# Reordering a pair's round in a fused attention and two-MLP kernel: evictions ahead of maxima, scores ahead of the next first mixing

## The chip, the cores and the metric

One core of a Trainium2 chip runs the whole program in one launch. The metric is the device time of a run in microseconds (us). Engines are called by their short names: PE (TensorE, matmuls), ACT (ScalarE), DVE (VectorE), POOL (GpSimd), and SP, which here only issues transfers. Each engine works through its own instructions in the order in which the program was written.

## The reference, cut to what matters

```python
# 4 batches, 12 heads, 448 positions, head size 64
scores = scale * np.matmul(q, k.transpose(0, 1, 3, 2))
scores = np.einsum('bhij,hg->bgij', scores, w_pre)       # first mixing of heads
scores = scores - np.max(scores, axis=-1, keepdims=True)
attn = np.exp(scores)
attn = attn / (np.sum(attn, axis=-1, keepdims=True) + 1e-09)
attn = np.einsum('bhij,hg->bgij', attn, w_post)          # second mixing of heads
out = np.matmul(attn, v)
# then a gated MLP with a token mixing (w_in, w_sg, w_out), then a second MLP
# (w_theta, w_tok, w_ch); w_in and the others come as 64-bit floats
```

## The kernel before, in words

The program has an attention stage and then two dense stages. Only the attention stage is touched. It is written out by hand, with no scheduler: the order of the Python calls is the order of instructions on every engine.

The 448 query rows of a batch make four tiles, of 120, 120, 120 and 88 rows. A tile is cut into blocks of 10 rows, and two blocks make a **pair**; the last tile of a batch ends in a single block of 8 rows. That is 6 + 6 + 6 + 5 = 23 pairs a batch, 92 in all. The main loop runs one **round** r per pair and works on several pairs at once, at different depths:

- *re-layout* for pair r+4: SP moves a pair's rows of all heads from the score tile `s` into two `blk` tiles (L216). Three sets of `blk` take turns, so the copy waits for the first mixing of three pairs earlier.
- *first mixing* (`premix`) for pair r+2: PE multiplies `blk` by `kpre` into two psB banks (L224). There are two psB buffers, so it waits for the exponentials of the pair before.
- *maxima* (`rowmax`, DVE, L230, `nmx`) and *exponentials* (`expo`, ACT, L238, `e`, each followed by a small read of its sum), then a reciprocal: first step on POOL (`recip`, L244), second on DVE (`recip2`, L249), both writing `rc`. `weigh` (POOL, L260) scales the second mixing's weights `wr` by it for pair r+1.
- *second mixing* (`postmix`) for pair r: PE, 64 small matmuls into two of three psC buffers (L282; L274 for a single).
- *evictions* of psC: `at_hi` on ACT (L305, tile `ah`, half precision) and `at_lo` on DVE (L311, tile `al`, the remainder `psC - ah`, so it needs `ah` first). A pair has two of each, e = 0 and 1.
- *scores* for a later tile (`scores`, PE, L200, into psA, which is one buffer of two banks) and their eviction on ACT (L206, tile `s`). A tile has six score steps, spread over the 6 or 5 rounds of the tile ahead; over 5 rounds one round gets two.
- *products with v* (`attn_v`, PE, L334, into psD, one bank), scaled by DVE (`out_x`, L342) and stored by SP (`store_x`, L347).

What doesn't run in each round is put into lists by round number and run from them: `early` (transfers), `work` (scores, products with v, two small matmuls `v_turn` L149 and `v_spread` L160 per batch that also write psA, `out_x`) and `late` (preparing the next batch's v: `v_max`, `v_mul` L172, `v_hi` L177, `v_lo` L181; and the decoding of `w_in`). Decoding is cut into 18 jobs (the argument `extra`), spread over rounds 1 to 84, one about every 4.7 rounds. A job has `words` in round r (ACT `dp` L568 and `dl` L569, then DVE `da` L571 and L573), `value` and `high` in r+1 (DVE L579; ACT `dh` L584, DVE L585) and `low` in r+2 (DVE L591, POOL L593).

Between a round's list `late` and the next round stands the second remainder, `at_lo(r, 1)`:

```python
            for fn, a in late.get(r, []):
                fn(*a)
            if live:
                at_lo(r, 1)
```

Of the kernel before, what the change touches and what calls it, by code (L numbers as in the profile page):

```python
# [6 lines left out]
F32 = mybir.dt.float32  # L7
# [3 lines left out]
U32 = mybir.dt.uint32  # L11
AF = mybir.ActivationFunctionType
ALU = mybir.AluOpType
# [11 lines left out]
LR, LQ = 4, 2  # L25
# [6 lines left out]
def attention(tc, nc, io, xT, B, extra, tail):  # L32
# [8 lines left out]
    NR = len(pairs)  # L41
# [7 lines left out]
    with ExitStack() as es:  # L49
# [5 lines left out]
        def pool_r(name, bufs, **kw):  # L55
            return early_es.enter_context(tc.tile_pool(name=name, bufs=bufs, side="right", reuse_waits="tile", **kw))
# [5 lines left out]
        dec = pool_r("a_dec", 1)  # L62
# [155 lines left out]
        def premix(r):  # L218
            ps = mix[r] = [psB.tile([128, 512], F32, tag="psB", name="psB") for _ in sblk[r]]
            for h in range(2):  # L220
                k = slice(64 * h, 64 * h + 64)
                for e, blk in enumerate(sblk[r]):
                    c = 64 * (h ^ e)
                    nc.tensor.matmul(ps[e][c:c + 64, :S], kpre[k, e], blk[k], start=True, stop=True)  # L224
            del sblk[r]

        def rowmax(r):
            nmx[r] = sm_p.tile([128, 2], F32, tag="nmx", name="nmx")
            for e, ps in enumerate(mix[r]):
                nc.vector.tensor_reduce(out=nmx[r][:, e:e + 1], in_=ps[:, :S], axis=AX.X, op=ALU.max, negate=True)  # L230
# [68 lines left out]
        def at_hi(r, e):  # L299
            b, t = pairs[r][:2]  # L300
            if e >= len(pc[r]):
                return
            if r == first[b, t] and e == 0:
                at[b, t] = [at_p.tile([128, 4 * H * TI], F16, tag=tag, name=tag) for tag in ("ah", "al")]
            nc.scalar.activation(out=at_view(r, e, at[b, t][0]), in_=at_src(r, e), func=AF.Copy, scale=2.0 ** -17)  # L305

        def at_lo(r, e):
            if e >= len(pc[r]):
                return
            ah, al = (at_view(r, e, x) for x in at[pairs[r][:2]])  # L310
            nc.vector.scalar_tensor_tensor(out=al, in0=at_src(r, e), scalar=2.0 ** -17, in1=ah,  # L311
                                           op0=ALU.mult, op1=ALU.subtract)
# [34 lines left out]
            nc.sync.dma_start(out=dst.rearrange("(c p) i -> p c i", p=128), in_=xs.pop((b, t, half))[:, :, :n])  # L347


        early, work, late = {}, {}, {}  # L350

        def put(d, r, fn, *a):
            d.setdefault(r, []).append((fn, a))
# [5 lines left out]
        for T in range(1, nt):  # L359
            b, t = tiles[T]  # L360
            u = units(T)
            for c in range(NP):
                put(work, u[c], scores, b, t, c)
            if T > 1:
                put(early, u[0] - QO, load_q, b, t)
            if t == 0:
                for c, r in enumerate(units(T - 1)):
                    put(early, r, load_k, b, c)
        for b in range(B):
            f = first[b, 0]  # L370
            g = min(f, 1)
            for c in range(NP):
                put(early, f - 9 + c if b else -4 + c // 2, load_v, b, c)
                put(late, f - 7 + c if b else -2 + c // 3, v_max, b, c)
                for d, fn in enumerate((v_mul, v_hi, v_lo)):
                    put(late, f + 2 - g + c + d, fn, b, c)
            put(work, f - g, v_turn, b)
            put(late, f - g, v_top, b)
            put(work, f + 1 - g, v_spread, b)
            put(late, f + 1 - g, v_scale, b)  # L380
        for T in range(nt):
            b, t = tiles[T]
            for c in range(NP):
                if T == nt - 1:
                    r = last[b, t] + 1 + c // 3
                else:
                    r = last[b, t] + min(1 + c, 5 if t == 2 else 6)
                put(work, r, attn_v, b, t, c)
                if c % 3 == 2:
                    put(work, r, out_x, b, t, c // 3)  # L390
                    put(early, r + 1, store_x, b, t, c // 3)

        for j, fn in enumerate(extra):
            r = JR0 + (NR - JR0 - JR1) * j // len(extra)
            put(early, r - 2, fn[0], dec)
            for d, i in ((0, 1), (1, 2), (1, 3), (2, 4)):
                put(late, r + d, fn[i], dec)
            put(early, r + 4, fn[5], dec)


# [16 lines left out]
        for r in range(-LR, NR + 7):  # L417
            live = 0 <= r < NR
            if 0 <= r + LR < NR:
                relayout(r + LR)  # L420
            for fn, a in early.get(r, []):
                fn(*a)
            if live:
                postmix(r)
            if 0 <= r + LQ < NR:
                premix(r + LQ)
            if 0 <= r + LQ - 1 < NR:
                recip2(r + LQ - 1)
                weigh(r + LQ - 1)
            if live:  # L430
                at_hi(r, 0)
                at_lo(r, 0)
                at_hi(r, 1)
            if 0 <= r + LQ < NR:
                rowmax(r + LQ)
                expo(r + LQ)
                recip(r + LQ)
            for fn, a in work.get(r, []):
                fn(*a)
            for fn, a in late.get(r, []):  # L440
                fn(*a)
            if live:
                at_lo(r, 1)
            if r == NR - LR - 1:
                early_es.close()
            for key in (2 * (r - NR), 2 * (r - NR) + 1):
                for fn in tail.get(key, []):
                    fn()
# [21 lines left out]
class Dense:  # L470
# [71 lines left out]
    def decode(self, src, n, dst, tiles=None):  # L542

        nc, box = self.nc, {}

        def block(pool, i):
            if tiles:
                return tiles(i)  # L550
            if i == 0:
                box["hl"] = pool.tile([128, 2, 256], F32R, tag="dh", name="dh", bufs=self.out_bufs)
            return box["hl"][:, i, :n]

        def load(pool):
            raw = pool.tile([128, 256, 2], U32, tag="draw", name="draw", bufs=self.raw_bufs)
            nc.sync.dma_start(out=raw.rearrange("p n w -> p (n w)")[:, :2 * n], in_=src.bitcast(U32))
            box["raw"] = raw

        def words(pool):  # L560
            raw = box["raw"]
            lo, hi = raw[:, :n, 0], raw[:, :n, 1]
            a, low, p = (pool.tile([128, 256], F32, tag=t, name=t, bufs=self.mid_bufs)[:, :n]
                         for t in ("da", "dl", "dp"))
            au = a.bitcast(U32)


            nc.scalar.activation(out=p, in_=hi.bitcast(F32), func=AF.Copy, scale=2.0 ** -112)  # L568
            nc.scalar.activation(out=low, in_=lo, func=AF.Copy, scale=2.0 ** -52)  # L569
            pu = p.bitcast(U32)  # L570
            nc.vector.tensor_scalar(out=au, in0=pu, scalar1=3, scalar2=0x7FFFFFF8,  # L571
                                    op0=ALU.logical_shift_left, op1=ALU.bitwise_and)
            nc.vector.scalar_tensor_tensor(out=au, in0=pu, scalar=0x80000000, in1=au,  # L573
                                           op0=ALU.bitwise_and, op1=ALU.bitwise_or)
            box.update(a=a, low=low, p=p)

        def value(pool):
            a, p = box["a"], box["p"]
            nc.vector.tensor_scalar(out=p.bitcast(U32), in0=a.bitcast(U32), scalar1=0xFF800000, scalar2=None,  # L579
                                    op0=ALU.bitwise_and)  # L580

        def high(pool):
            h = block(pool, 0)
            nc.scalar.activation(out=h, in_=box["a"], func=AF.Copy)  # L584
            nc.vector.tensor_tensor(out=box["p"], in0=box["p"], in1=box["low"], op=ALU.mult)  # L585
            box["h"] = h

        def low(pool):
            a, p, h = (box[k] for k in ("a", "p", "h"))
            lo = block(pool, 1)  # L590
            nc.vector.tensor_tensor(out=a, in0=a, in1=h.bitcast(F32), op=ALU.subtract)  # L591
            eng = nc.vector if self.mid_bufs > 1 else nc.gpsimd
            eng.tensor_tensor(out=lo, in0=a, in1=p, op=ALU.add)  # L593
            box["lo"] = lo

        def store(pool):
            if tiles:
                return
            nc.sync.dma_start(out=dst, in_=box["hl"][:, :, :n].bitcast(F32))

        return load, words, value, high, low, store

    def decode_tiles(self, src, rows, c0, c1, tiles):
# [669 lines left out]
```

## Time and profile before

| what | value |
|---|---|
| median of 3 runs | 1001.59 us (1000.46 to 1003.74) |
| the profiled execution: its own time | 1002.4 us |
| its span, first to last instruction | 1000.5 us |
| busy over the span: PE, DVE, ACT, POOL | 92%, 68%, 53%, 25% |
| mean granted TensorE clock | 0.971 of full speed |

Times in the rows below are us from the span's start. A round shows best on ACT: it begins with the pair of `ah` evictions, of which most rounds have one row with x2. Counted so, round 0 begins at 30.77, round 4 at 52.87 and round 83 at 426.16. A row of the timeline has start, duration, engine, line, operation, output <- input, and in brackets how long the engine had been idle and what it waited for. Rows that follow each other closely overlap a little, since an engine starts an instruction before the one ahead has left it; the distance between two starts is what an instruction costs its engine. A row of the windows view has from:to, its length, then the busy time (and instructions) of PE, PE's weight loads, DVE, ACT and POOL, then the granted TensorE clock, the DMA engines' busy share and GB/s.

### The profile page before, as it was taken

Reading aid. Unit: us, or ns where it says so; the run is one execution under the profiler, and the core shown is the slowest. Engines: PE = TensorE matmul, PEld = TensorE weight load, DVE = VectorE, ACT = ScalarE, POOL = GpSimd, SP = SyncE. Lnnn points to the kernel's source line nnn. Section 1 sums busy time; section 2 is a strip of 40 time slices with the busy share of each in tenths; the row PEclk is TensorE's granted clock in tenths of the full one; section 3 lists DMA queues with packets and bytes.
Section 4 is the critical chain, followed back from the end, with each engine's and each line's share of the span. In section 5 each row is a group of like instructions: output and inputs, shape, how many; then the busy total and the mean of one; then the engine's idle time right before and its main releaser. Section 6 shows DMA issues by size and latency. Waiting matters only on the chain.

```text
span 1000.5 us, 28660 instructions
## 1 busy us (share of the span) xinstructions
PE 918.6 (92%) x11632; PEld 687.9 (69%) x11632; DVE 679.3 (68%) x1512; ACT 525.7 (53%) x1188; POOL 248.9 (25%) x450
## 2 busy tenths in 40 slices
PE   6888979988898978996989999998998999999998
PEld 2344545544554545555868888887988999999997
DVE  2576657756675757773999898976987737837521
ACT  4577657766576757763755546443553404513310
POOL 0152215311251225320000000001460623622611
PEclk9799989999899999998999999999999999999999
DMA  5537644666347634458635857679762031030111
GB/s 165 168 122 212 181 161 149 187 173 185 105 151 202 191 118 150 142 121 267 200 104 171 283 166 218 195 250 329 220 212 82 26 102 49 26 102 16 56 56 56
DMA packets 126963, 151.80 MB, mean 152 GB/s; under 512 B 26352, under 2 KB 112624, under 8 KB 126832
## 3 DMA queue, kind: packets, MB, share of 16 engines
q1 hardware_dynamic: 126832, 149.97, 48.2%
q8 instruction: 92, 1.51, 0.6%
q14 instruction: 39, 0.32, 0.1%
HBM read 79.09 MB, written 32.31 MB: 111 GB/s over the span
## 4 chain that ended last, share of the span: by engine, by line
PE 48%; DVE 21%; ACT 20%; issue 5%; DMA 4%; SPq 1%; ACTq 0%; DVEq 0%
PE ps L533 39%; ACT e L238 9%; ACT s L206 6%; DVE nmx L230 5%; DVE al L311 4%; ACT ah L305 3%; PE psC L282 2%; PE psD L334 2%; PE psB L224 2%; DMA blk<-s 2%; PE psA L200 1%; DVE da L573 1%; DVE da L571 1%; DMA win<-win_d 1%; DVE r L1043 1%
## 5 line engine op out<-in xcount | busy, mean ns | idle before, releaser
L238 ACT ACTIVATE e<-psB,nmx 128x448 f32<-128x448 f32 x180 | 112.6, 630 | 101.2 <-DVE nmx L230 98.5
L311 DVE SCALAR_TENSOR_TENSOR al<-psC,ah 128x480 f16<-128x480 f32 x180 | 116.6, 649 | 53.1 <-ACT ah L305 53.0
L224 PE MATMUL psB<-blk,kpre 64*64 64x448 f32 x720 | 128.4, 579 | 7.6 <-DMA blk<-s 3.3
L282 PE MATMUL psC<-wr,e 64*64 64x60 f32 x5632 | 109.7, 228 | 12.5 <-POOL wr L260 8.9
L282 PEld LDWEIGHTS psC<-wr,e 64*64 64x64 f32 x5632 | 97.0, 141 | 25.6 <-POOL wr L260 13.4
L230 DVE TENSOR_REDUCE nmx<-psB 128x1 f32<-128x448 f32 x180 | 103.4, 615 | 13.0 <-PE psB L224 12.8
L305 ACT ACTIVATE ah<-psC 128x480 f16<-128x480 f32 x180 | 93.1, 576 | 33.3 <-PE psC L282 33.3
L200 PE MATMUL psA<-k,q 64*120 64x448 f32 (+1 forms) x384 | 99.4, 599 | 9.8 <-ACT s L206 9.8
L529 POOL TENSOR_TENSOR x2s<-x,x2s 128x384 fp32r<-128x384 f32 x28 | 29.6, 1079 | 308.5 <-ACT x2s L526 308.5
L533 PE MATMUL ps<-wtok,z 128*128 128x448 f32 x504 | 104.8, 368 | 0.4 <-POOL z L529 0.4
L533 PEld LDWEIGHTS ps<-wtok,z 128*128 128x128 f32 x504 | 94.4, 188 | 10.0 <-POOL z L529 0.8
L334 PEld LDWEIGHTS <-vh 128*64 128x64 f16 x1536 | 61.2, 117 | 58.1 <-issue 58.0
L533 PE MATMUL ps<-wth,x2s 128*128 128x384 f32 x504 | 93.7, 342 | 3.2 <-POOL x2s L529 1.7
L533 PEld LDWEIGHTS ps<-wth,x2s 128*128 128x128 f32 x504 | 88.7, 191 | 3.9 <-POOL x2s L529 2.0
L533 PE MATMUL ps<-u,wch 128*128 128x448 f32 x432 | 89.9, 368 | 0.0
L206 ACT ACTIVATE s<-psA 120x896 f32<-120x896 f32 (+1 forms) x90 | 82.1, 912 | 14.0 <-PE psA L200 14.0
L533 PEld LDWEIGHTS ps<-u,wch 128*128 128x128 f32 x432 | 81.0, 188 | 8.1
L200 PEld LDWEIGHTS psA<-k,q 64*120 64x120 f32 (+1 forms) x384 | 27.5, 176 | 79.7 <-ACT s L206 61.5
L529 POOL TENSOR_TENSOR z<-zz,z 128x384 fp32r<-128x384 f32 x56 | 61.9, 1125 | 72.4 <-ACT z L526 72.2
L260 POOL TENSOR_SCALAR wr<-w,rc 128x60 f32<-128x60 f32 x180 | 54.9, 320 | 91.1 <-DVE rc L249 61.2
L244 POOL TENSOR_SCALAR rc<-sum 128x2 f32<-128x2 f32 (+1 forms) x92 | 19.4, 211 | 220.2 <-ACT e L238 217.5
L334 PE MATMUL psD<-ah,vh 128*64 128x120 f16 (+1 forms) x768 | 70.9, 229 | 0.0
(126 smaller groups left out, 1600.0 us busy)
## 6 DMA issues: line engine op xcount, KB each, us to landing
blk<-s SPq DMA_DIRECT2D x176, 210.0 KB
vraw<-in_vN SPq DMA_DIRECT2D x24, 256.0 KB
draw<-in_w_in SPq DMA_DIRECT2D x24, 256.0 KB
k<-in_kvT SPq DMA_DIRECT2D x24, 224.0 KB
xraw<-xT SPq DMA_DIRECT2D x24, 224.0 KB
xres<-xT SPq DMA_DIRECT2D x24, 224.0 KB
x2T<-xres SPq DMA_DIRECT2D x24, 224.0 KB
xres<-x2T SPq DMA_DIRECT2D x24, 224.0 KB
```

Of the source, the lines that this page charges most:

```text
L200: nc.tensor.matmul(ps[e][:n, :S], q[p, o:o + n], k[p], start=True, stop=True)
L206: nc.scalar.activation(out=out, in_=pair[:n, :, :S], func=AF.Copy, scale=0.125)
L224: nc.tensor.matmul(ps[e][c:c + 64, :S], kpre[k, e], blk[k], start=True, stop=True)
L230: nc.vector.tensor_reduce(out=nmx[r][:, e:e + 1], in_=ps[:, :S], axis=AX.X, op=ALU.max, negate=True)
L238: nc.scalar.activation(out=x, in_=ps[:, :S], func=AF.Exp, bias=m[:, e:e + 1], accum_out=sm[:, e:e + 1])
L260: nc.gpsimd.tensor_scalar(out=w, in0=wts[n], scalar1=rc[:, e:e + 1], scalar2=0.0, op0=ALU.mult, op1=ALU.add)
L282: nc.tensor.matmul(pc[r][h][c:c + 64, jc, :, SQ * e:SQ * e + SQ], x[p, c:c + 64], wr[r][e][p], start=(e == 0 and jc == 0), stop=(e == 1 an ...
L305: nc.scalar.activation(out=at_view(r, e, at[b, t][0]), in_=at_src(r, e), func=AF.Copy, scale=2.0 ** -17)
L311: nc.vector.scalar_tensor_tensor(out=al, in0=at_src(r, e), scalar=2.0 ** -17, in1=ah, op0=ALU.mult, op1=ALU.subtract)
L334: nc.tensor.matmul(ps[p, o:o + n], v[:, jc, p], a[:, i0:i0 + n], start=(o == 0 and m == 0), stop=(o > TI and m == len(terms) - 1))
L529: eng.tensor_tensor(out=out, in0=in_, in1=hi.bitcast(F32), op=ALU.subtract)
L533: self.nc.tensor.matmul(ps, l, r, start=(i == 0), stop=(i == len(terms) - 1))
```

## The change

The body of a round is written in another order. The second remainder follows the first at once, ahead of the maxima. The first score step of a round moves out of `work` into a new list `front`, which runs ahead of the first mixing. A second new list, `mid`, runs at the same place and takes ACT's and POOL's steps of the decoding, and POOL's steps for v; DVE's steps of both stay in `late`, and `out_x` joins them there. `words`, `high` and `low` are cut into two parts by engine for this, and `value` moves from round r+1 to round r. The work itself is the same.

```diff
-                put(work, u[c], scores, b, t, c)
+                put(front if u[c] not in u[:c] else work, u[c], scores, b, t, c)
...
-                for d, fn in enumerate((v_mul, v_hi, v_lo)):
-                    put(late, f + 2 - g + c + d, fn, b, c)
+                put(mid, f + 3 - g + c, v_mul, b, c)
+                put(late, f + 3 - g + c, v_hi, b, c)
+                put(mid, f + 4 - g + c, v_lo, b, c)
...
-                    put(work, r, out_x, b, t, c // 3)
+                    put(late, r, out_x, b, t, c // 3)
...
-            for d, i in ((0, 1), (1, 2), (1, 3), (2, 4)):
-                put(late, r + d, fn[i], dec)
+            words, value, high, low = fn[1:5]
+            for i in range(2):
+                put((mid, late)[i], r, words, dec, i)
+                put((mid, late)[i], r + 1, high, dec, i)
+            put(late, r, value, dec)
+            put(late, r + 1, low, dec, 0)
+            put(mid, r + 2, low, dec, 1)
...
             if live:
                 postmix(r)
-            if 0 <= r + LQ < NR:
-                premix(r + LQ)
             if 0 <= r + LQ - 1 < NR:
                 recip2(r + LQ - 1)
                 weigh(r + LQ - 1)
             if live:
-                at_hi(r, 0)
-                at_lo(r, 0)
-                at_hi(r, 1)
+                for e in range(2):
+                    at_hi(r, e)
+                    at_lo(r, e)
+            for d in (front, mid):
+                for fn, a in d.get(r, []):
+                    fn(*a)
             if 0 <= r + LQ < NR:
+                premix(r + LQ)
                 rowmax(r + LQ)
                 expo(r + LQ)
                 recip(r + LQ)
-            for fn, a in work.get(r, []):
-                fn(*a)
-            for fn, a in late.get(r, []):
-                fn(*a)
-            if live:
-                at_lo(r, 1)
+            for d in (work, late):
+                for fn, a in d.get(r, []):
+                    fn(*a)
...
-        def high(pool):
-            h = block(pool, 0)
-            nc.scalar.activation(out=h, in_=box["a"], func=AF.Copy)
-            nc.vector.tensor_tensor(out=box["p"], in0=box["p"], in1=box["low"], op=ALU.mult)
-            box["h"] = h
+        def high(pool, part=None):
+            if part != 1:
+                box["h"] = block(pool, 0)
+                nc.scalar.activation(out=box["h"], in_=box["a"], func=AF.Copy)
+            if part != 0:
+                nc.vector.tensor_tensor(out=box["p"], in0=box["p"], in1=box["low"], op=ALU.mult)
```

Where the instructions come to stand is seen best on three engines. First ACT, over three rounds with a decoding job in the second batch; `dp`, `dl` and `dh` are the job's. Before:

```order
L206 ACTIVATE s<-psA 120x896
L568 ACTIVATE dp<-draw 128x256
L569 ACTIVATE dl<-draw 128x256
L305 ACTIVATE ah<-psC 128x48x10 x2
L238 ACTIVATE e,sum<-psB,nmx 128x448 x2
L206 ACTIVATE s<-psA 120x896
L584 ACTIVATE dh<-da 128x256
L305 ACTIVATE ah<-psC 128x48x10 x2
L238 ACTIVATE e,sum<-psB,nmx 128x448 x2
```

Of the change:

```order
L305 ACTIVATE ah<-psC 128x48x10 x2
L206 ACTIVATE s<-psA 120x896
L570 ACTIVATE dp<-draw 128x256
L571 ACTIVATE dl<-draw 128x256
L238 ACTIVATE e,sum<-psB,nmx 128x448 x2
L305 ACTIVATE ah<-psC 128x48x10 x2
L206 ACTIVATE s<-psA 120x896
L587 ACTIVATE dh<-da 128x256
L238 ACTIVATE e,sum<-psB,nmx 128x448 x2
```

The score eviction and the decoding copies stood behind the exponentials, at the end of a round; now they stand between the `ah` evictions and the exponentials.

Then DVE, over two rounds at about the same place; `nmx` are the maxima, `rc` the reciprocal. Before:

```order
L230 TENSOR_REDUCE nmx<-psB 128x1 x2
L571 TENSOR_SCALAR da<-dp 128x256
L573 SCALAR_TENSOR_TENSOR da<-dp,da 128x256
L311 SCALAR_TENSOR_TENSOR al<-psC,ah 128x48x10
L249 RECIPROCAL rc<-rc 128x2
L311 SCALAR_TENSOR_TENSOR al<-psC,ah 128x48x10
L230 TENSOR_REDUCE nmx<-psB 128x1 x2
L342 TENSOR_TENSOR x<-psD,dsc 128x3x88
L177 CAST vh<-vraw 128x512
```

Of the change:

```order
L230 TENSOR_REDUCE nmx<-psB 128x1 x2
L177 CAST vh<-vraw 128x512
L574 TENSOR_SCALAR da<-dp 128x256
L576 SCALAR_TENSOR_TENSOR da<-dp,da 128x256
L581 TENSOR_SCALAR dp<-da 128x256
L249 RECIPROCAL rc<-rc 128x2
L311 SCALAR_TENSOR_TENSOR al<-psC,ah 128x48x10 x2
L230 TENSOR_REDUCE nmx<-psB 128x1 x2
```

Before, one of the two remainders stood behind the extra work of its round and ahead of the next reciprocal; now both stand together between the reciprocal and the maxima.

Last PE, at the end of a batch, in the round of the single block (L274) in which `v_turn` (psV, L149) is due. Before:

```order
L274 MATMUL psC<-wr,e 128x12x8 x4
L224 MATMUL psB<-blk_123,kpre 64x448
L224 MATMUL psB<-blk_124,kpre 64x448
L224 MATMUL psB<-blk_123,kpre 64x448
L224 MATMUL psB<-blk_124,kpre 64x448
L200 MATMUL psA<-k,q 120x448 x2
L149 MATMUL psV<-ident,vmx 6x128
```

Of the change:

```order
L274 MATMUL psC<-wr,e 128x12x8 x4
L200 MATMUL psA<-k,q 120x448 x2
L224 MATMUL psB<-blk_123,kpre 64x448
L224 MATMUL psB<-blk_124,kpre 64x448
L224 MATMUL psB<-blk_123,kpre 64x448
L224 MATMUL psB<-blk_124,kpre 64x448
L149 MATMUL psV<-ident,vmx 6x128
```

The scores moved from behind the first mixing to ahead of it, so that the first mixing now stands between them and the small matmul that writes the same psA.

## Rows read from the trace of the kernel before

**Rows 1.** Windows view, rounds 4 to 82: busy us (instructions) by engine, clock, DMA.

```profile
53.00:426.00 373.00, 332.89 (x7771) 187.66 (x7768) 249.38 (x568) 258.85 (x598) 118.75 (x299) 0.96 0.53 162
```

**Rows 2.** Timeline of ACT, one plain round.

```profile
91.80 1.03 ACT L305 ACTIVATE ah<-psC 128x480 f16<-128x480 f32 x2
93.70 0.63 ACT L238 ACTIVATE e<-psB,nmx 128x448 f32<-128x448 f32 x1 [0.87 <-DVE nmx L230]
...
94.33 0.63 ACT L238 ACTIVATE e<-psB,nmx 128x448 f32<-128x448 f32 x1
...
94.94 0.90 ACT L206 ACTIVATE s<-psA 88x896 f32<-88x896 f32 x1
95.74 1.02 ACT L305 ACTIVATE ah<-psC 128x480 f16<-128x480 f32 x2
```

**Rows 3.** Timeline of DVE, the same round.

```profile
92.40 0.66 DVE L311 SCALAR_TENSOR_TENSOR al<-psC,ah 128x480 f16<-128x480 f32 x1 [0.81 <-ACT ah L305]
92.97 1.15 DVE L230 TENSOR_REDUCE nmx<-psB 128x1 f32<-128x448 f32 x2
...
95.36 0.17 DVE L249 RECIPROCAL rc<-rc 128x2 f32<-128x2 f32 x1 [0.67 <-POOL rc L244]
```

**Rows 4.** Timeline of PE, one round in which little is waited for.

```profile
73.20 1.16 PE L282 MATMUL psC<-wr,e 64*64 64x60 f32 x64 [0.53 <-POOL wr L260]
74.18 0.96 PE L224 MATMUL psB<-blk,kpre 64*64 64x448 f32 x8
75.07 0.99 PE L200 MATMUL psA<-k,q 64*88 64x448 f32 x4
...
76.74 1.16 PE L282 MATMUL psC<-wr,e 64*64 64x60 f32 x64
```

**Rows 5.** Timeline of ACT, two rounds with steps of a decoding job.

```profile
78.55 1.02 ACT L305 ACTIVATE ah<-psC 128x480 f16<-128x480 f32 x2
...
83.14 1.03 ACT L305 ACTIVATE ah<-psC 128x480 f16<-128x480 f32 x2
...
87.86 1.02 ACT L305 ACTIVATE ah<-psC 128x480 f16<-128x480 f32 x2
```

**Rows 6.** Timeline of PE and ACT, end of the first batch (rounds 14, 22, 23).

```profile
104.29 1.04 ACT L305 ACTIVATE ah<-psC 128x480 f16<-128x480 f32 x2 [1.92 <-PE psC L282]
134.15 0.50 ACT L305 ACTIVATE ah<-psC 128x384 f16<-128x384 f32 x1
138.07 0.59 PE L149 MATMUL psV<-ident,vmx 128*6 128x128 f32 x2 [2.63 <-ACT s L206]
142.34 1.03 ACT L305 ACTIVATE ah<-psC 128x480 f16<-128x480 f32 x2 [4.33 <-PE psC L282]
148.89 1.04 ACT L305 ACTIVATE ah<-psC 128x480 f16<-128x480 f32 x2 [2.50 <-PE psC L282]
```

**Rows 7.** Windows view, behind the wait at 138.07; columns as in rows 1.

```profile
138.00:142.00 4.00, 3.93 (x107) 3.35 (x111) 0.72 (x3) 0.02 (x1) 0.00 (x0) 0.61 0.20 76
```

**Rows 8.** Timeline of ACT: rounds 0, 4, 83 and 84; from round 83 on no scores.

```profile
30.77 1.03 ACT L305 ACTIVATE ah<-psC 128x480 f16<-128x480 f32 x2 [0.81 <-PE psC L282]
...
52.87 1.04 ACT L305 ACTIVATE ah<-psC 128x480 f16<-128x480 f32 x2
...
426.16 1.02 ACT L305 ACTIVATE ah<-psC 128x480 f16<-128x480 f32 x2
...
429.30 1.04 ACT L305 ACTIVATE ah<-psC 128x480 f16<-128x480 f32 x2
```

**Rows 9.** Timeline of POOL and DVE: a decoding step beside POOL's work, and alone.

```profile
174.03 1.17 POOL L181 TENSOR_TENSOR vl<-vraw,vh 128x512 f16<-128x512 f32 x1
174.84 0.51 DVE L571 TENSOR_SCALAR da<-dp 128x256 uint32<-128x256 uint32 x1 [1.76 <-ACT dp L568]
153.65 0.29 DVE L571 TENSOR_SCALAR da<-dp 128x256 uint32<-128x256 uint32 x1 [2.10 <-ACT dp L568]
```

**Rows 10.** Tile view of blk: idle time of engines until its transfers (us, times).

```profile
  DMA blk<-s: 4.5, 5
```

More of the change, by code (lines that the diff above doesn't have):

```diff
@@ L347, in store_x @@
             nc.sync.dma_start(out=dst.rearrange("(c p) i -> p c i", p=128), in_=xs.pop((b, t, half))[:, :, :n])
-        early, work, late = {}, {}, {}
+        early, front, mid, work, late = {}, {}, {}, {}, {}
         def put(d, r, fn, *a):
@@ L558, in load, with words @@
             box["raw"] = raw
-        def words(pool):
+        def words(pool, part=None):
             raw = box["raw"]
[L562 to L575, printed above, removed]
+            if part != 1:
+                for t in ("a", "low", "p"):
+                    box[t] = pool.tile([128, 256], F32, tag="d" + t[0], name="d" + t[0], bufs=self.mid_bufs)[:, :n]
+                nc.scalar.activation(out=box["p"], in_=raw[:, :n, 1].bitcast(F32), func=AF.Copy, scale=2.0 ** -112)
+                nc.scalar.activation(out=box["low"], in_=raw[:, :n, 0], func=AF.Copy, scale=2.0 ** -52)
+            if part != 0:
+                au, pu = (box[t].bitcast(U32) for t in "ap")
+                nc.vector.tensor_scalar(out=au, in0=pu, scalar1=3, scalar2=0x7FFFFFF8,
+                                        op0=ALU.logical_shift_left, op1=ALU.bitwise_and)
+                nc.vector.scalar_tensor_tensor(out=au, in0=pu, scalar=0x80000000, in1=au,
+                                               op0=ALU.bitwise_and, op1=ALU.bitwise_or)
         def value(pool):
@@ L580, in value, with low @@
                                     op0=ALU.bitwise_and)
-        def high(pool):
-            h = block(pool, 0)
-            nc.scalar.activation(out=h, in_=box["a"], func=AF.Copy)
-            nc.vector.tensor_tensor(out=box["p"], in0=box["p"], in1=box["low"], op=ALU.mult)
-            box["h"] = h
-        def low(pool):
-            a, p, h = (box[k] for k in ("a", "p", "h"))
[L590 to L594, printed above, removed]
+        def high(pool, part=None):
+            if part != 1:
+                box["h"] = block(pool, 0)
+                nc.scalar.activation(out=box["h"], in_=box["a"], func=AF.Copy)
+            if part != 0:
+                nc.vector.tensor_tensor(out=box["p"], in0=box["p"], in1=box["low"], op=ALU.mult)
+        def low(pool, part=None):
+            a, p, h = (box[k] for k in ("a", "p", "h"))
+            if part != 1:
+                box["lo"] = block(pool, 1)
+                nc.vector.tensor_tensor(out=a, in0=a, in1=h.bitcast(F32), op=ALU.subtract)
+            if part != 0:
+                eng = nc.vector if self.mid_bufs > 1 else nc.gpsimd
+                eng.tensor_tensor(out=box["lo"], in0=a, in1=p, op=ALU.add)
         def store(pool):
```

## The prediction

> **What bounds the kernel now.** I looked first at how busy the engines are over the stretch that the change touches, rounds 4 to 82. No engine is full: DVE works 249 of 373 us, ACT 259, and PE's 333 hold waits too, as shown below [rows 1]. DMA is at 0.53. So the stage is bound by a loop of waits between engines, and the next view has to be the timeline of one round, on the engine that shows it best.
>
> A plain round on ACT lasts from one pair of `ah` evictions to the next, 95.74 - 91.80 = 3.94 us, and ACT idles 0.87 of it, for the maxima [rows 2]. DVE meanwhile idles 0.81 for `ah` [rows 3]. Read together these give a closed loop of starts: `ah` 91.80, first `al` 92.40 (0.60 later), `nmx` 92.97 (0.57), first `e` 93.70 (0.73), second `e` 94.33 (0.63), `s` 94.94 (0.61), next `ah` 95.74 (0.80). 0.60 + 0.57 + 0.73 + 0.63 + 0.61 + 0.80 = 3.94: nothing else is in a plain round's length.
>
> PE's own work in a round is shorter: with nothing to wait for but the start, second mixing, first mixing, scores and a product with v take 76.74 - 73.20 = 3.54 us (0.98, 0.89, and 1.67 for the last two) [rows 4]. In most rounds it stretches to fill 3.94.
>
> 79 rounds, 4 to 82, take 426.16 - 52.87 = 373.3 us [rows 8], where 79 x 3.94 would be 311.3. The other 62 us are of two kinds. A round with `dp` and `dl` lasts 83.14 - 78.55 = 4.59, the one behind it, with `dh`, 87.86 - 83.14 = 4.72 [rows 5]: 0.65 + 0.78 = 1.43 over plain, and 17 of the 18 jobs lie in the stretch, 24.3 us. And at the end of a batch three rounds are long [rows 6]: round 14 with two score steps, from 95.74 [rows 2] to 104.29, 8.55; round 22 with `v_turn`, 142.34 - 134.15 = 8.19; round 23 with `v_spread`, 148.89 - 142.34 = 6.55. Over plain that is 4.61 + 4.25 + 2.61 = 11.47, three times 34.4. What the three share is a second use of psA in one round: PE stands before it until ACT has evicted the scores (2.63 for `v_turn` [rows 6]), and what it does next runs slow: behind that wait the granted clock is 0.61 on average, partly at 1.2 GHz instead of 2.4 [rows 7]. 24.3 + 34.4 leaves 3 of the 62 unexplained.
>
> **The change, part by part.** *Plain rounds.* The score eviction leaves the loop (-0.80): it now stands in the idle time before the exponentials. The second `al` enters it (+0.57, the step from `al` to the next DVE instruction) since it now precedes the maxima. The new loop is `ah` 0.60 `al` 0.57 `al` 0.57 `nmx` 0.73 `e` 0.63 `e` 0.61 `ah` = 3.71 [rows 2, 3]. Does it hold? Four things have to arrive in time. (a) Between the evictions' start and the first `e` ACT has 0.60 + 0.57 + 0.57 + 0.73 = 2.47; two `ah` take about 1.0, `s` 0.80: 0.67 is left over. (b) Scores take 0.99 on PE behind the second mixing, so they are done when both `ah` are. (c) The first mixing, now behind the scores, can start when the second `e` has freed psB, that is as `ah` starts, and takes 0.95; the maxima want it 0.60 + 0.57 + 0.57 = 1.74 behind that. PE, with 3.54, can stay ahead by some 0.8 and so be in time. (d) The reciprocal on DVE comes 95.36 - 94.33 = 1.03 behind the start of the second `e` and takes 0.17, to 1.20; the first `al` starts 0.61 + 0.60 = 1.21 behind that. It is just in time, and stands in front of both `al`. So 3.94 - 3.71 = 0.23 a round, 79 x 0.23 = **-18.2**. At one end stands PE's 3.54 (-31.6); at the other end, if PE is late with the first mixing, nothing is gained (0). I take the loop, since each of its steps has a row.
>
> *Decoding.* `dp` and `dl`, the only additions to the ACT part of their round, cost it 0.65 (4.59 - 3.94 [rows 2, 5]), and `dh`, one copy of the same size, about half of that; both fit the 0.67 of (a). DVE's `da` waited 2.10 for `dp` [rows 9] with a remainder and the reciprocal behind it; now `dp` is done before the maxima. Work in `late` has from the maxima's end (2.47 - 0.73 + 1.15 = 2.9 behind `ah`) to the next reciprocal (2.47 + 0.63 + 1.03 = 4.1, by (d)), 1.2 us; the three steps `da`, `da`, `dp` take about 1.0 at the pace of [rows 9] and fit, but not with a step of v or `out_x` in the same round, so I leave 0.2 a job: 24.3 - 3.4 = **-20.9**, with bounds 0 and -24.3.
>
> *Ends of batches.* The wait for psA goes, because `s` is evicted some 1.9 behind the start of the round, when PE is still at the first mixing. What is left is PE's own extra work: in round 14 a second score step (0.99) and up to 0.7 of waiting for psA, since that one stays behind the first mixing; in rounds 22 and 23 a small matmul and a second product with v, about 0.7 each. I take 3 a batch: 34.4 - 9 = **-25.4**, bounds 0 and -34.4. What is late next there is PE itself, not a wait.
>
> *Rounds without scores.* From round 83 a round lasted 429.30 - 426.16 = 3.14 [rows 8], the loop without `s`. The second `al` lengthens these to 3.71. Five such rounds: **+2.9**.
>
> *POOL beside DVE.* POOL's steps for v now stand between `wr` and `rc`, so they run beside the maxima and the late DVE work, and `v_hi` waits for the `v_mul` of its own round. `da` took 0.51 beside POOL's `vl` and 0.29 alone [rows 9]. 18 rounds (6 for each of three batches) at about 0.17: **+3**, bounds 0 and +21 (each time a whole `vl`).
>
> The Trainium skill says more than that row: in the page SBUF — State Buffer, section "SBUF: two separate sides", GpSimd and VectorE share one pair of ports, and an instruction of one that needs the pair blocks the other for its whole length. By that rule a DVE step that meets `vl` (1.17) could lose all of it, and the sum would be some 18 us higher. The row shows a loss of 0.22, a part of that length.
>
> *Start.* Rounds 0 to 3 took 52.87 - 30.77 = 22.1, waiting for psC at first [rows 8]. At 3.71 they would take 14.8; I take nothing, bound -7.3. Behind the attention stage all is as before and only begins earlier.
>
> Sum: -18.2 - 20.9 - 25.4 + 2.9 + 3 = -58.6. The profiled execution took 1002.4 us, 0.8 above the median of the three runs; 1001.6 - 58.6 = **943 us**, 5.9% less.
>
> **Rivals.** *All is hidden.* Ends of batches and decoding cost nothing and the start shrinks: 943 - 9 - 3.4 - 3 - 7.3 = 920. For it: PE's work is 3.54. Against: round 14 has 0.99 more of it. I give 0.12.
>
> *The first mixing binds.* If PE doesn't get ahead, the maxima come later by what the scores take, and a plain round stays at 3.94: 943 + 18.2 = 961. For it: PE has only 3.71 - 3.54 = 0.17 to spare and a second product with v costs 0.68. 0.20.
>
> *The port.* DVE's late work stands still for one whole POOL step of v in each of the 18 rounds, and the loop with it: 18 x 1.17 (`vl` [rows 9]) = 21, of which 3 are counted: 943 + 18 = 961. Against: `da` lost 0.22 and not 1.17 there. For it speaks that `da` did lose something beside `vl`. This is where the Trainium skill's rule, taken in full, would lead. 0.09.
>
> *Slower: SP's queue.* `out_x` moves to the end of DVE's round, so the store that needs it waits longer on SP, and the re-layout copies of the next pair queue behind it. The copies run two rounds ahead (7.4 us), and before, engines waited for them 4.5 us in all, 5 times [rows 10]. There are 32 stores; if each held the copies 2.0 us beyond that lead, 64 us would go: 943 + 64 = 1007. It decides only once a store's wait and a copy's own time exceed 7.4; a store can wait about one round, 3.7. 0.06. That the change does nothing is excluded by the order in which instructions now stand; that its gains cancel is left 0.03.
>
> **How the numbers follow.** The forecast has 0.50, with a range of its own from 930 to 955. From 920 (all hidden) to 975 (the first mixing's 18 us and most of the port's together) the cases hold 0.50 + 0.20 + 0.09 and half of the 0.12, some 0.85. A change within 0.3% (3 us) can't be told from none with these runs. Only the SP case is slower (0.06), cancelling gains are "same" (0.03), the rest is faster (0.91).
>
> **What would show it.** On ACT: plain rounds of 3.71 with an idle of about 0.67 before the first `e`, still for `nmx`; rounds with `dp`, `dl` or `dh` hardly longer; rounds 14, 22 and 23 below 6; rounds from 83 on longer than 3.14. On PE: no wait for `s` before L149 or L160, and fewer stretches of low clock. On DVE: no wait of `da` for `dp`. I am wrong if plain rounds stay near 3.94 (then look at what the maxima wait for: PE), if `e` waits for DVE that works through late steps or idles beside POOL, or if the first mixing waits for `blk`.

## The result and the profile after

The changed kernel takes 932.6 us (median of 4 runs, 931.2 to 938.0) against 1001.6 of the kernel before; the ratio is 0.932, 95% interval 0.928 to 0.936. That is 69 us less, where 59 were forecast, and inside the range. The profiled execution has a span of 929.4 us and took 931.2. Rounds 4 to 82 took 307.3 us in place of 373.3.

The windows view of these rounds in the changed kernel (columns as in [rows 1]):

```profile
48.09:355.38 307.29, 300.96 (x7766) 175.80 (x7764) 251.74 (x568) 258.63 (x601) 118.90 (x298) 1.00 0.64 197
```

Every engine runs the same instructions as in [rows 1], and DVE, ACT and POOL are busy as long as before, within 1%. What went is waiting, and on PE also time at the lower clock: its busy time fell from 333 to 301 us while the granted clock rose from 0.96 to 1.00. PE is now busy 98% of the stretch; that alone doesn't make it the limit, as the run with few products shows below. DMA's share rose from 0.53 to 0.64.

A plain round, from the timeline of ACT and of DVE (to lay beside [rows 2, 3]):

```profile
78.15 1.03 ACT L305 ACTIVATE ah<-psC 128x480 f16<-128x480 f32 x2
79.05 0.92 ACT L206 ACTIVATE s<-psA 88x896 f32<-88x896 f32 x1
80.62 0.64 ACT L238 ACTIVATE e<-psB,nmx 128x448 f32<-128x448 f32 x1 [0.66 <-DVE nmx L230]
...
81.86 1.03 ACT L305 ACTIVATE ah<-psC 128x480 f16<-128x480 f32 x2
```

```profile
78.56 0.17 DVE L249 RECIPROCAL rc<-rc 128x2 f32<-128x2 f32 x1
78.75 1.22 DVE L311 SCALAR_TENSOR_TENSOR al<-psC,ah 128x480 f16<-128x480 f32 x2
79.89 1.14 DVE L230 TENSOR_REDUCE nmx<-psB 128x1 f32<-128x448 f32 x2
```

The round lasts 81.86 - 78.15 = 3.71, as worked out: the two `al` stand together (78.75 to 79.89), `s` runs between `ah` and `e`, and ACT idles 0.66 before the first `e`.

Rounds with decoding, rounds 14, 22 and 23, and the first rounds without scores, all on ACT (beside [rows 5, 6, 8]):

```profile
70.75 1.03 ACT L305 ACTIVATE ah<-psC 128x480 f16<-128x480 f32 x2
...
72.45 0.44 ACT L570 ACTIVATE dp<-draw 128x256 f32<-128x256 f32 x1
...
74.44 1.04 ACT L305 ACTIVATE ah<-psC 128x480 f16<-128x480 f32 x2
...
76.14 0.43 ACT L587 ACTIVATE dh<-da 128x256 fp32r<-128x256 f32 x1
...
85.56 1.03 ACT L305 ACTIVATE ah<-psC 128x480 f16<-128x480 f32 x2
...
90.36 1.04 ACT L305 ACTIVATE ah<-psC 128x480 f16<-128x480 f32 x2 [0.17 <-PE psC L282]
...
119.67 0.49 ACT L305 ACTIVATE ah<-psC 128x384 f16<-128x384 f32 x1
...
123.92 1.03 ACT L305 ACTIVATE ah<-psC 128x480 f16<-128x480 f32 x2 [1.01 <-PE psC L282]
...
127.95 1.04 ACT L305 ACTIVATE ah<-psC 128x480 f16<-128x480 f32 x2
...
355.38 1.03 ACT L305 ACTIVATE ah<-psC 128x480 f16<-128x480 f32 x2
...
359.09 1.04 ACT L305 ACTIVATE ah<-psC 128x480 f16<-128x480 f32 x2
```

A round with `dp` and `dl` lasts 74.44 - 70.75 = 3.69, the next, with `dh`, 78.15 - 74.44 = 3.71: here decoding is hidden. Where `dh` meets a step of v in the same round (rounds 6, 30, 53 and 76) the round lasts 3.97 to 3.99, where it was 5.3. Round 14 lasts 4.80 (8.55 before), round 22 4.25 (8.19), round 23 4.03 (6.55). Without scores a round lasts 3.71 (3.14 before).

The two other signs that the prediction named hold in the main. PE waits 0.21 before L149 in round 22 (2.63 before [rows 6]) and 0.10 before L160 in round 23 (2.45 before), and DVE's `da` waited for `dp` 19 times before, 30.1 us in all, and now waits 3 times, 2.8 us:

```profile
121.02 0.38 PE L149 MATMUL psV<-ident,vmx 128*6 128x128 f32 x2 [0.21 <-ACT s L206]
```

One wait is new. In round 19, which lasts 6.94, the score eviction stands 3.23 us, and in the next round `dh` 0.97:

```profile
105.31 1.03 ACT L305 ACTIVATE ah<-psC 128x480 f16<-128x480 f32 x2
109.57 0.92 ACT L206 ACTIVATE s<-psA 120x896 f32<-120x896 f32 x1 [3.23 <-PE psC L282]
...
112.25 1.03 ACT L305 ACTIVATE ah<-psC 128x480 f16<-128x480 f32 x2
115.06 0.42 ACT L587 ACTIVATE dh<-da 128x256 fp32r<-128x256 f32 x1 [0.97 <-DMA win_d<-dh]
```

PE's `psC`, named in the first bracket, had ended before; this is the first eviction into a score tile whose last re-layout copy was issued one round earlier, so a transfer is most likely what it waits for. The same eviction one and two batches later (rounds 42 and 65) waits 2.4 and 0.9, and there a transfer is named. These waits differ between executions: in the second profile of the same kernel (a0_after, below) the three are 2.2, 2.7 and 2.2, and the one of 2.7 names the copy itself, `blk<-s`.

### The profile page after: what moved, and what is told of

Its sections match the earlier page's. It is cut to its first block, busy times and chain, and to the rows that moved or that the text cites. A ratio compares the mean times of both kernels' runs of the same rounds, so it can differ in the third digit from the quotient of the medians.

```text
span 929.4 us, 28674 instructions
## 1 busy us (share of the span) xinstructions
PE 886.8 (95%) x11632; PEld 677.9 (73%) x11632; DVE 681.2 (73%) x1512; ACT 525.2 (57%) x1188; POOL 249.0 (27%) x450
## 4 chain that ended last, share of the span: by engine, by line
PE 66%; DVE 15%; DMA 6%; ACT 6%; issue 3%; POOL 2%; SPq 1%; ACTq 0%; DVEq 0%; POOLq 0%
PE ps L538 44%; PE psC L282 6%; PE psA L200 5%; PE psB L224 5%; PE psD L334 4%; ACT e L238 3%; DVE al L311 2%; DMA blk<-s 2%; DVE nmx L230 1%; ACT s L206 1%; DMA vraw<-in_vN 1%; DMA win<-win_d 1%; ACT ah L305 1%; DVE da L576 1%; PE ps L1032 1%
## 5 line engine op out<-in xcount | busy, mean ns | idle before, releaser
L311 DVE SCALAR_TENSOR_TENSOR al<-psC,ah 128x480 f16<-128x480 f32 x180 | 109.3, 648 | 8.2 <-ACT ah L305 7.2
L534 POOL TENSOR_TENSOR x2s<-x,x2s 128x384 fp32r<-128x384 f32 x28 | 29.9, 1089 | 307.6 <-ACT x2s L531 307.6
L224 PE MATMUL psB<-blk,kpre 64*64 64x448 f32 x720 | 103.6, 565 | 5.5 <-DMA blk<-s 2.6
L282 PE MATMUL psC<-wr,e 64*64 64x60 f32 x5632 | 104.2, 222 | 1.1 <-POOL wr L260 0.7
L200 PE MATMUL psA<-k,q 64*120 64x448 f32 (+1 forms) x384 | 96.8, 579 | 7.3 <-ACT s L206 5.8
L282 PEld LDWEIGHTS psC<-wr,e 64*64 64x64 f32 x5632 | 92.2, 135 | 12.6 <-POOL wr L260 5.7
L334 PEld LDWEIGHTS <-vh 128*64 128x64 f16 x1536 | 57.0, 111 | 56.9 <-issue 56.7
L224 PEld LDWEIGHTS psB<-blk,kpre 64*64 64x64 f32 x720 | 24.7, 131 | 70.0 <-ACT e L238 46.9
L538 PE MATMUL ps<-g,wout 128*128 128x448 f32 x288 | 63.3, 378 | 5.7 <-DVE g L534 3.3
```

What stands on the lines that cost most here:

```text
L200: nc.tensor.matmul(ps[e][:n, :S], q[p, o:o + n], k[p], start=True, stop=True)
L282: nc.tensor.matmul(pc[r][h][c:c + 64, jc, :, SQ * e:SQ * e + SQ], x[p, c:c + 64], wr[r][e][p], start=(e == 0 and jc == 0), stop=(e == 1 an ...
L334: nc.tensor.matmul(ps[p, o:o + n], v[:, jc, p], a[:, i0:i0 + n], start=(o == 0 and m == 0), stop=(o > TI and m == len(terms) - 1))
L534: eng.tensor_tensor(out=out, in0=in_, in1=hi.bitcast(F32), op=ALU.subtract)
L538: self.nc.tensor.matmul(ps, l, r, start=(i == 0), stop=(i == len(terms) - 1))
```

## The experiments

Each was made from the changed kernel, except the one that says otherwise. Ratios are to the kernel before, run beside each group (medians of 1001.0 us for the labels with a, 1000.4 with b, 999.8 with d), with 95% intervals. By these intervals two versions that differ by less than some 3 us can't be told apart.

**The changed kernel again** (label a0_after), the measure for the runs below. 

> The changed kernel again, as the measure for the runs beside it: 931 to 938 us, plain rounds of 3.71 us on ACT. No theory expects anything else.

 Measured: 933.1 us, ratio to the kernel before 0.9326 (0.9305 to 0.9346).

**The second remainder behind the maxima** (a1_al2_behind_maxima):

```diff
-                for e in range(2):
-                    at_hi(r, e)
-                    at_lo(r, e)
+                at_hi(r, 0)
+                at_lo(r, 0)
+                at_hi(r, 1)
...
                 recip(r + LQ)
+            if live:
+                at_lo(r, 1)
             for d in (work, late):
```

> Of the change one thing is undone: the second remainder (al, e = 1) goes behind the maxima again, but ahead of the late work; scores, decoding and v stay as changed. If the plain round of 3.71 us is the loop of ACT and DVE (ah 0.60, al 0.57, al 0.57, nmx 0.73, e 0.63, e 0.61), the loop loses 0.57 and PE's own 3.54 to 3.6 us becomes the round; rounds without scores go from 3.71 back to 3.14. That is 79 x 0.1 to 0.17 plus 5 x 0.57, less what late work on DVE now delays: 918 to 926 us. If PE, which reaches the first mixing only behind the scores, sets the 3.71, plain rounds stay at 3.71 and the time at 929 to 934 us.

 Measured: 927.2 us, ratio 0.9256 (0.9230 to 0.9282), 5.9 us less than the changed kernel (some 3 either way), the lowest of all versions that leave no work out, and just above what was expected. Rounds without scores went back to 3.15, but rounds 89 and 90 then wait longer for the next stage's loads, so that hardly anything of this is left at round 91; the gain lies in rounds 4 to 82 (301.1 us, against 307.3 and 309.0 in the two profiles of the changed kernel). Plain rounds fell only to 3.67, and the timelines of ACT and DVE show why:

```profile
78.89 1.03 ACT L305 ACTIVATE ah<-psC 128x480 f16<-128x480 f32 x2
...
82.56 1.03 ACT L305 ACTIVATE ah<-psC 128x480 f16<-128x480 f32 x2
```

```profile
80.58 1.16 DVE L230 TENSOR_REDUCE nmx<-psB 128x1 f32<-128x448 f32 x2 [0.44 <-PE psB L224]
```

The maxima now wait for the first mixing: PE sets this round. Its timeline, in the round before:

```profile
73.87 1.16 PE L282 MATMUL psC<-wr,e 64*64 64x60 f32 x64
74.96 0.99 PE L200 MATMUL psA<-k,q 64*88 64x448 f32 x4
75.88 0.98 PE L224 MATMUL psB<-blk,kpre 64*64 64x448 f32 x8
77.54 1.16 PE L282 MATMUL psC<-wr,e 64*64 64x60 f32 x64
```

PE needs 77.54 - 73.87 = 3.67 with no wait, not the 3.54 of [rows 4]: in the new order the second mixing takes 1.09 to the next start, where it took 0.98.

**The scores back behind the exponentials** (a2_scores_back):

```diff
-                put(front if u[c] not in u[:c] else work, u[c], scores, b, t, c)
+                put(work, u[c], scores, b, t, c)
```

> Of the change one thing is undone: all score steps go back behind the first mixing and the exponentials, the two remainders stay together ahead of the maxima. By the loop of ACT and DVE the score eviction comes back into it (+0.80): plain rounds of 4.51 us, 79 x 0.80 = 63 us more, and the waits for psA at the ends of batches come back in part (+15 to +25): 1005 to 1025 us, slower than before the change. If instead the gain came from the remainders and the split decoding alone, plain rounds stay below 3.94 and the time below 960 us.

 Measured: 1016.0 us, ratio 1.0151 (1.0133 to 1.0168): 1.5% slower than before the change, as the loop says. Its plain round on ACT:

```profile
93.48 1.03 ACT L305 ACTIVATE ah<-psC 128x480 f16<-128x480 f32 x2
...
97.18 0.90 ACT L206 ACTIVATE s<-psA 88x896 f32<-88x896 f32 x1
97.98 1.02 ACT L305 ACTIVATE ah<-psC 128x480 f16<-128x480 f32 x2
```

97.98 - 93.48 = 4.50, with `s` again as the round's last step; round 14 is 9.1 (8.55 before the change).

**The decoding back at the rounds' end** (a3_decode_back):

```diff
-            words, value, high, low = fn[1:5]
-            for i in range(2):
-                put((mid, late)[i], r, words, dec, i)
-                put((mid, late)[i], r + 1, high, dec, i)
-            put(late, r, value, dec)
-            put(late, r + 1, low, dec, 0)
-            put(mid, r + 2, low, dec, 1)
+            for d, i in ((0, 1), (1, 2), (1, 3), (2, 4)):
+                put(late, r + d, fn[i], dec)
```

> Of the change one thing is undone: the 18 decoding jobs run at the end of rounds as before (words in r, value and high in r+1, low in r+2, all in late). If the split was worth what the rows of before say, each job costs again 0.65 for dp and dl, 0.31 for dh, and 0.1 to 0.4 of DVE's wait for dp: 18 x 1.06 to 1.4 = 19 to 25 us more, 951 to 958 us. If the new order of the round hides decoding wherever it stands, less than 6 us more.

 Measured: 943.4 us, ratio 0.9417 (0.9393 to 0.9441): 10.4 us more, between the two. ACT's timeline has the two rounds of a job:

```profile
72.70 1.03 ACT L305 ACTIVATE ah<-psC 128x480 f16<-128x480 f32 x2
...
77.09 1.00 ACT L305 ACTIVATE ah<-psC 128x480 f16<-128x480 f32 x2
...
81.06 1.02 ACT L305 ACTIVATE ah<-psC 128x480 f16<-128x480 f32 x2
```

4.39 and 3.97, 0.68 and 0.26 over 3.71. The copies `dp` and `dl` cost what was counted; the round with `dh` costs a third of its 0.78 before. Together that is 0.94 for a job.

**POOL's v steps back behind `rc`** (b1_v_back):

```diff
-                put(mid, f + 3 - g + c, v_mul, b, c)
-                put(late, f + 3 - g + c, v_hi, b, c)
-                put(mid, f + 4 - g + c, v_lo, b, c)
+                for d, fn in enumerate((v_mul, v_hi, v_lo)):
+                    put(late, f + 2 - g + c + d, fn, b, c)
```

> Of the change one thing is undone: POOL's two steps for v (v_mul, v_lo) stand behind the reciprocal's first step at the end of a round again. If the port that POOL and DVE share cost the forecast 3 us or more in the new place, this is 2 to 4 us faster than the changed kernel. If the place matters through the weights wr, which POOL then scales only behind 1.9 us of v work, PE starts its second mixing late in the 18 rounds with v work, by about 0.4 each: 3 to 8 us slower. Port by the whole length of a step (21 us): about 18 us faster.

 Measured: 933.1 us, ratio 0.9314 (0.9285 to 0.9343): no difference from the changed kernel. So the place of POOL's steps costs nothing that can be told here, neither by the port nor by the weights. The run moves these steps and doesn't take them away, so it doesn't say what POOL beside DVE costs in either place.

**The loads of v four rounds earlier** (b2_v_loads_early): `f - 9 + c` in the line of `load_v` becomes `f - 13 + c`. 

> The changed kernel with the loads of the next batch's v issued four rounds earlier (rounds 10 to 15 of a batch in place of 14 to 19). In rounds 19, 42 and 65 of the changed kernel the first score eviction of a tile waits 3.2, 2.4 and 0.9 us for transfers (it writes the score tile whose last re-layout copy was issued one round before), and once dh waits 1.0. If the v loads beside those copies make them late, the waits go and the time falls by 5 to 8 us, to 924 to 929. If the copies are late by their own place in SP's queue, the waits stay and the time with them.

 Measured: 936.0 us, ratio 0.9344 (0.9320 to 0.9369): no gain. The wait of round 19 is gone (0.44), but round 14 has one now, 7.87 us long where it was 4.80. ACT, and the windows view of rounds 10 to 13, 14 and 16 to 20:

```profile
86.28 1.02 ACT L305 ACTIVATE ah<-psC 128x480 f16<-128x480 f32 x2
88.76 0.92 ACT L206 ACTIVATE s<-psA 120x896 f32<-120x896 f32 x1 [1.46 <-DMA blk<-s]
...
94.15 1.04 ACT L305 ACTIVATE ah<-psC 128x480 f16<-128x480 f32 x2 [2.22 <-PE psC L282]
```

```profile
71.47:86.28 14.81, 14.81 (x402) 8.70 (x400) 11.83 (x26) 13.15 (x34) 3.86 (x13) 1.00 0.94 264
86.28:94.15 7.87, 5.55 (x104) 3.53 (x104) 3.06 (x7) 4.09 (x11) 1.58 (x6) 0.78 0.85 245
97.95:116.34 18.39, 18.39 (x498) 10.83 (x498) 16.95 (x37) 16.01 (x39) 4.75 (x16) 1.00 0.61 167
```

The loads of v and those of k fall into the same rounds there, and DMA's share reached 0.94; in round 14 the clock fell to 0.78 as well.

**The loads of v two a round, from round 14** (d1_v_loads_paired): the same line with `f - 9 + c // 2`. 

> The changed kernel with the six loads of the next batch's v in rounds 14, 14, 15, 15, 16, 16 of a batch in place of 14 to 19, so that none stands just ahead of a tile's first score eviction (rounds 14 and 19). If v loads beside the last re-layout copy of a score tile make that eviction wait, the waits of 2 to 3 us in rounds 19, 42 and 65 go and don't come back in rounds 14, 37 and 60: 4 to 8 us faster than the changed kernel, 925 to 929 us. If the copies are late by SP's queue or by DMA load as such, waits of the same sum remain and the time is 931 to 937.

 Measured: 937.1 us, ratio 0.9367 (0.9338 to 0.9397), some 4 us more than the changed kernel, which is hardly beyond the noise, although no load of v stands just ahead of round 19 any more. Its eviction waits 4.47:

```profile
105.23 1.03 ACT L305 ACTIVATE ah<-psC 128x480 f16<-128x480 f32 x2
110.73 0.92 ACT L206 ACTIVATE s<-psA 120x896 f32<-120x896 f32 x1 [4.47 <-PE psB L224]
```

The theory that a load of v next to the copy delays it falls. Other loads still stand there: SP issues those of q and `w_in` at 101.22 and 101.87 and the copy at 103.83. The second theory, that the load on SP's queue or on DMA as a whole does it, is left.

**Both, with the second remainder behind the maxima** (b4_al2_and_v_loads, loads four rounds earlier; d2_al2_and_v_paired, loads in twos). 

> The changed kernel with both edits: the second remainder behind the maxima and the v loads four rounds earlier. If each acts on its own (loop of ACT and DVE; transfers at the ends of batches), the gains add: 912 to 921 us. If PE sets the plain round, only the loads' part is left, 924 to 929.

 Measured: 932.3 us, ratio 0.9319 (0.9293 to 0.9346). 

> The same loads together with the second remainder behind the maxima. If the two gains are independent (5.9 us measured for the remainder, 4 to 8 for the loads): 918 to 924 us, the fastest so far. If the remainder's gain only fills the wait for transfers, 925 to 930.

 Measured: 929.4 us, ratio 0.9298 (0.9268 to 0.9327). Both miss: the loads bring nothing to add. Each is still faster than the same loads without the remainder's move (936.0 and 937.1), by 3.7 and 7.7, the first of which is within the noise.

**The scores alone** (b3_scores_only), made from the kernel before: the list `front` with the first score step of a round runs ahead of the first mixing and of the exponentials, all else as before. 

> The kernel before with one part of the change alone: the first score step of a round runs ahead of the first mixing and is evicted ahead of the exponentials; the second remainder stays at the end of the round and decoding and v as before. By the loop of ACT and DVE (3.94 without the eviction's 0.80 is 3.14) plain rounds fall to PE's 3.54 to 3.6, and the waits for psA at the ends of batches go: 1001.5 - 79 x 0.35 - 25 = 949 us, 940 to 960. If the moves only work together, it stays above 980.

 Measured: 940.9 us, ratio 0.9401 (0.9362 to 0.9441). This one move, of the scores on PE and of their eviction on ACT, brings 59 of the 69 us. Plain rounds come down to 3.15 on ACT where PE allows it, with longer ones between:

```profile
71.39 1.03 ACT L305 ACTIVATE ah<-psC 128x480 f16<-128x480 f32 x2
...
75.70 1.03 ACT L305 ACTIVATE ah<-psC 128x480 f16<-128x480 f32 x2
...
79.63 1.03 ACT L305 ACTIVATE ah<-psC 128x480 f16<-128x480 f32 x2
...
82.78 1.04 ACT L305 ACTIVATE ah<-psC 128x480 f16<-128x480 f32 x2
```

Rounds 10 and 11 have the decoding's 4.31 and 3.93, round 12 is 3.15. Over the 31 rounds of 4 to 82 that have no decoding, no end of a batch and no wait for transfers the mean is 3.62 (3.94 before, 3.74 in the changed kernel), near the 3.54 to 3.6 that were expected of PE.

**Few products with v** (d3_changed_few_products and, from the version with the remainder behind the maxima, d4_al2_few_products):

```diff
             o = TI * (c % 3)
+            terms = terms[:1]
             for m, (v, jc, a) in enumerate(terms):
```

> The changed kernel with 22 of the 24 matmuls of each product with v left out, so that PE has about 0.65 us less per round; evictions, scaling and stores stay, and the values are wrong in the output. If the plain round of 3.71 is the loop of ACT and DVE, it stays at 3.70 to 3.72; only rounds that PE sets (two score steps, ends of batches, those of 3.78) shorten: 918 to 928 us. If PE set it, plain rounds fall to 3.1 to 3.3 and the time below 900.

 Measured: 921.6 us, ratio 0.9222 (0.9191 to 0.9253). Plain rounds on ACT are unchanged:

```profile
78.19 1.03 ACT L305 ACTIVATE ah<-psC 128x480 f16<-128x480 f32 x2
...
81.90 1.04 ACT L305 ACTIVATE ah<-psC 128x480 f16<-128x480 f32 x2
...
85.60 1.03 ACT L305 ACTIVATE ah<-psC 128x480 f16<-128x480 f32 x2
```

3.71 and 3.70 with some 0.6 us less work on PE (a product goes from 0.75 to 0.17): the loop of ACT and DVE holds the changed kernel's plain round by itself. The rounds of 3.78 to 3.80, which had been expected to shorten, didn't (rounds 7 and 8 are 3.79 and 3.78), so PE doesn't set them. In rounds 7 and 8 of the changed kernel `vh` waits 0.42 for POOL's `v_mul`, which stands behind `vl`.

> The same cut in the version with the second remainder behind the maxima, where PE's own 3.67 us should set the round. Without the products PE needs about 3.0 and the loop of ACT and DVE 3.14: plain rounds of 3.15 to 3.25 us, 880 to 900 us. If something other than PE holds that version at 3.67, rounds stay above 3.5 and the time above 912.

 Measured: 910.8 us, ratio 0.9104 (0.9068 to 0.9140). Here the same cut shortens plain rounds, so PE had set them:

```profile
79.61 1.03 ACT L305 ACTIVATE ah<-psC 128x480 f16<-128x480 f32 x2
...
82.80 1.03 ACT L305 ACTIVATE ah<-psC 128x480 f16<-128x480 f32 x2
```

3.19 in place of 3.67. The whole is 11 us above the upper end of what was expected: rounds with a step of decoding, of v or of `out_x` on DVE stayed at 3.5 to 3.8, and the waits for transfers at the ends of batches grew (4.6 us in round 19).

## Why the prediction was right

*The loop of a plain round* was right to the hundredth: 3.71 forecast, 3.71 measured, and shown to be that loop from three sides. Leaving PE's work out doesn't shorten it (d3), bringing the score eviction back makes it 4.50 (a2), and taking the second `al` out of it shortens it until PE is next (a1). The price of the second `al` is 5.9 us of the whole; the gain of 0.80 for `s` carries the change.

*The first mixing binds*: this rival came closer than its 18 us say. Step (c) took PE's round as 3.54 from [rows 4], where the first mixing follows the second. In the new order, with the scores between them, PE needs 3.67. So PE could not run 0.8 ahead for free; it has 0.04 to spare in a plain round. It was enough for the forecast, but moving the second remainder back then saves only 0.04 in a plain round like the one shown; over the 31 ordinary rounds it is 0.12 on average (3.74 to 3.62), since behind rounds that are longer for another reason PE is ahead and the next is shorter (3.53 in round 9 behind two of 3.8), and 0.08 to 0.10 over all of rounds 4 to 82, where 0.1 to 0.17 were expected of a1.

*Decoding* was counted at -20.9, by one job of before; the 14 jobs that meet neither an end of a batch nor a wait for transfers cost 22.9 us before (1.64 each, more than 1.43, since those with a step of v beside them cost 2.0) and cost 2.1 now, 20.8 less. That this meets the term is luck: the term stood for 17 jobs at 1.23 each, and the other three lie in rounds that now wait for transfers. Undoing its part of the change in the new order costs only 10.4, since there a job at the end of the round costs 0.94 and not 1.43 (a3). So about half of the term is no gain of the split but of the order of the round. The sum of terms was safe from this, since it compared old rounds with new ones; the label on the term was not.

*Ends of batches*: rounds 14, 22 and 23 are 4.80 + 4.25 + 4.03 - 3 x 3.71 = 1.95 over plain, where I had left 3. All nine such rounds lay 35.8 over plain before, not the 34.4 that the first batch gave times three, and lie 5.9 over it now: 29.9 less, where 25.4 were counted. Not foreseen was the wait for transfers in rounds 19, 42 and 65 (3.2, 2.4 and 0.9): moving the eviction forward in its round moved it closer to the copy that it has to wait for. I had weighed SP's queue only for the first mixing, where little happened: engines waited for `blk` 5.1 us in all, 4.5 before [rows 10].

*Rounds without scores* became longer as forecast.

*POOL beside DVE* was counted at +3 and measured at nothing that can be told (b1), though 3 us would be at the edge of the noise. The rounds in which v is prepared (24 and not 18, since the first batch has its six as well) and the one behind each six lie 2.0 us over plain in all, decoding included. The term was small because of where the steps fell, and not because a DVE step loses little beside POOL. In the changed kernel each of the 24 `vl` runs beside `al` and `nmx`, which read PSUM and keep their 0.65 and 0.61. Only `vh` is lengthened, four times, and beside another step of POOL, the decoding's `dh`:

```profile
62.79 0.72 POOL L598 TENSOR_TENSOR dh<-da,dp 128x256 fp32r<-128x256 f32 x1
62.85 0.94 DVE L177 CAST vh<-vraw 128x512 f16<-128x512 f32 x1 [0.42 <-POOL vraw L172]
```

With a median of 0.43, `vh` lost 0.51 of the 0.66 us that `dh` still had to run. The prediction read [rows 9] wrongly in this: `da` began when `vl` had 0.36 left, and lost 0.22 of that, not of 1.17. The rule of the Trainium skill (SBUF — State Buffer, "SBUF: two separate sides"), by which the instruction that has the ports blocks the other for its whole length, is borne out here but for some 0.15 us each time. In b3 a `da` that began when `vl` had 0.98 left took 1.26 in place of 0.43.

*Where the other 10 us came from.* In the profiled executions the span fell by 71.1: 66.0 in rounds 4 to 82 (61.5 of the terms belong there), 4.8 before round 4, of which I had taken nothing (29.01 and 48.09 are the starts of rounds 0 and 4 now, in place of 30.77 and 52.87), 2.3 from round 83 to round 91 where 2.9 more were forecast, and 2.0 lost later. The 66.0 are 18.2 in plain rounds, 29.9 at the ends of batches and 20.8 in the 14 jobs, less 2.9 in the other rounds, above all by the new waits. So the terms that were off are the ends of batches, POOL, the start, and the last rounds, whose waits for the next stage's loads also shrank (6.2 us before, 2.0 now). That the sum came so near is in part luck: the new waits for transfers, of which it has nothing, took back most of what the ends of batches gave beyond their term. And the start is the gain of one execution; in a0_after round 4 begins at 50.37, 2.5 earlier than before and not 4.8.

*Open*: how much of the delay of round 18's copy arises on SP and how much in the DMA engines. In round 19 DMA's share is 0.80, and from round 14 on SP issues without a pause, two copies taking it up to 2.8 us where they took 1.7; no run here takes one away without the other. The single packets in the trace show that a part lies behind SP: the copy is issued from 103.09 to 103.83, yet hardly any packet of its kind (1792 bytes, one row of a `blk`) moves before 105.45, while packets of 512 and 2048 bytes do, which are those of the loads of v and `w_in` issued ahead of it. `out_x`'s move was not tried by itself.

## What to carry to other kernels

Write a round's length as a closed chain of starts over the engines, and look for a step that nobody in a plain round waits for but that stands in the chain by its place in an engine's queue; moving that one (here the scores and their eviction, 59 of 69 us alone) was worth more here than everything moved along with it. Then check each companion move against the same chain: the second remainder, moved ahead of the maxima, cost 5.9 us (a1). And when a step moves forward in its round, look at what it waits for as well as at who waits for it, transfers included.

## What the runs showed of the hardware that I had not expected

The time of a block of matmuls on PE depends on its neighbours: the second mixing took 0.98 us to the next start with the first mixing behind it [rows 4] and 1.09 with the scores behind it (73.87 to 74.96 above), the whole round 3.54 and 3.67, at full granted clock both times. It is no accident of one round: at full clock and with no wait the median is 0.98 over 54 rounds of the kernel before and 1.09 over 76 of the changed one, and a1 has both, 1.09 in its rounds with scores and 0.98 in six without.

A DVE step that copies or combines tiles in SBUF (`vh`, `da`) and begins while a step of POOL runs lost what that one still had to run, less some 0.15 us: 0.22 of 0.36 [rows 9], 0.51 of 0.66 (above), 0.62 of 0.73 (b1) and 0.83 of 0.98 (b3). Steps that read PSUM (`al`, `nmx`) and the small reciprocal `rc` lost nothing beside the same steps of POOL.
